# An event list that sets the order of every instruction of a fused attention and two-MLP kernel

## The chip, the cores and the metric

The kernel runs on one NeuronCore of a Trainium2 chip. The metric is the device time of one execution in microseconds (us). The engines are TensorE (PE in the profile, its weight loads PEld), VectorE (DVE), ScalarE (ACT), GpSimd (POOL) and SyncE (SP), which issues most transfers.

## What is computed

Windowed attention with 8 global keys and a window of 96 over 2 x 8 heads of 768 tokens of 64 elements, then a gated MLP of 2048 inner columns and a second one of 1536. Tokens are 1536, the model width is 512.

```python
scores = scale * np.matmul(q, k.transpose(0, 1, 3, 2)) + bias[None, :, :, :]
scores = np.where(keep, scores, -1000000000.0)
a = np.exp(scores - np.max(scores, axis=-1, keepdims=True))
x = np.matmul(a / (np.sum(a, axis=-1, keepdims=True) + 1e-09), v)   # then [tokens, 512]
h = x @ w_in;  y = (h * sigmoid(h)) @ w_out
z = (sigmoid(y @ w_gate) * (y @ w_val)) @ moe2_w_out
```

The weights come as 64-bit floats. Each MLP product is made of three matmuls of a 32-bit kind (high by high, high by low, low by high).

## The kernel before, in words

Attention works on 12 blocks of 128 tokens and, in each, on 4 pairs of heads: 48 steps n. A step transposes a pair's queries and keys (`emit_T`, two transposes of 128x128, L342), evicts them to the key tile kt (L353 on VectorE or L355 on ScalarE), makes the scores (`emit_QK`, L379: two matmuls, each in one half of the rows of the array, 64*128; each stands as two records in the trace), reduces them with a mask (`soft`, L394 on VectorE), exponentiates (L401, ScalarE), normalises (L407, L408 on VectorE, L413 on GpSimd), transposes the weights of the values (`emit_PT`, L430, evicted at L434) and multiplies with the values (`emit_PV`, L451, each in one half of the columns, 128*64). `take` (L459) evicts a finished block of tokens to X, a high part on ScalarE and a low part on VectorE.

A weight tile is loaded raw (`dma_w`, L176), made 32-bit on ScalarE and VectorE (`to_f32`, L156 to L161), and split into a high and a low part (L169, L170). `pump_w` spaces these out by a count of units; tiles w0 to w15 exist from the start, w16 to w23 only after attention's memory is given back.

The MLP's matmuls all go through `mm3` (L505) or L682 and L684. While attention runs, `window` (L599) puts ten macros of the first MLP between attention's units. The table PLAN lists them as (token group, first inner chunk, columns, first column, attention slots); four have 256 columns, six have 512. A macro makes 24 matmuls into the inner banks H, then an activation, then 24 into the output bank Y (one bank, bank 7, evicted by VectorE at L589 and L591 to acc). `phase_rest` (L632) does the rest of both MLPs. Before any macro, `run_att` (L622) runs six units of attention alone and puts three warm-up matmuls on a tile of zeros (`warm_up`, L895) after each.

What sets the order: the code is written in the order of these units, and the framework's scheduler, which works with its own estimate of durations, then orders the instructions of each engine. Only for later score and value matmuls is TensorE's order given by hand (`tc.manual_schedule`, in `att_units`, L477). Tiles come from pools, and the framework adds the waits.

Of the kernel before, what the change touches and what calls it, by code (L numbers as in the profile page):

```python
# [8 lines left out]
F32 = mybir.dt.float32  # L9
# [16 lines left out]
NEG = 1.0e30  # L26
# [4 lines left out]

@with_exitstack
def attn_moe_moe2_kernel(
# [14 lines left out]
    nc = tc.nc  # L48
    B, H, S, D = q.shape
# [15 lines left out]
    stage_p = fast.enter_context(tc.tile_pool(name="stage", bufs=3))  # L65
    u_p = fast.enter_context(tc.tile_pool(name="up", bufs=2))
    g_p = fast.enter_context(tc.tile_pool(name="gp", bufs=4))
    e_p = fast.enter_context(tc.tile_pool(name="ep", bufs=2))
# [10 lines left out]
    nc.gpsimd.memset(pad, 0.0)  # L79
    W = [main.tile([128, 2, 512], F32R, name=f"w{n}") for n in range(16)]  # L80

# [71 lines left out]
    def to_f32(st, raw):  # L153
        lw, hw = raw[:, :, 0], raw[:, :, 1]
        ui = st.bitcast(I32)
        nc.scalar.activation(out=st, in_=hw.bitcast(F32), func=AF.Copy, scale=2.0 ** -112)  # L156
        nc.vector.tensor_scalar(ui, ui, 3, None, op0=ALU.logical_shift_left)
        nc.vector.scalar_tensor_tensor(  # L158
            out=ui, in0=lw, scalar=29, in1=ui, op0=ALU.logical_shift_right, op1=ALU.bitwise_or
        )  # L160
        nc.vector.scalar_tensor_tensor(  # L161
# [3 lines left out]
    def split_w(n):  # L165
        w = W[n % 24]
        st = u_p.tile([128, 512], F32, tag="u", name="u")
        to_f32(st, stages.pop(n))
        nc.scalar.activation(out=w[:, 0, :], in_=st, func=AF.Copy)  # L169
        nc.vector.tensor_tensor(w[:, 1, :], st, w[:, 0, :].bitcast(F32), ALU.subtract)  # L170

    def load_raw(st, s):
        o = st.rearrange("p f t -> p (f t)")
        if len(s.shape) == 3:
            o = o.rearrange("p (a f) -> p a f", f=256)
        nc.sync.dma_start(out=o, in_=s)  # L176

    def dma_w(n):
        st = stage_p.tile([128, 512, 2], I32, tag="stage", name="stage")
# [34 lines left out]
    qk_p = att.enter_context(tc.tile_pool(name="qkp", bufs=2))  # L214
    v_p = att.enter_context(tc.tile_pool(name="vp", bufs=3))
    t_p = att.enter_context(tc.tile_pool(name="tp", bufs=5))
    pt_p = att.enter_context(tc.tile_pool(name="ptp", bufs=3))
# [3 lines left out]
    ssum = [ap1.tile([128, 2], F32, name=f"ssum{i}") for i in range(4)]  # L221

    def load_n():
        raw = ap1.tile([128, 2, 2], I32, name="nraw")
        nc.sync.dma_start(out=raw[:, 0, :], in_=n_global.bitcast(I32).partition_broadcast(128))
        nc.scalar.dma_start(out=raw[:, 1, :], in_=n_local.bitcast(I32).partition_broadcast(128))
        return raw

    def make_n(raw):
        f = ap1.tile([128, 2, 2], F32, name="nf")  # L230
        neg = ap1.tile([128, 2, 1], F32, name="nneg")
        nc.vector.tensor_copy(f, raw)
        nc.vector.tensor_scalar(neg, f[:, :, 0:1], 0.0, None, op0=ALU.is_lt)
        nc.vector.tensor_tensor(neg, neg, f[:, :, 1:2], ALU.add)
        nc.vector.scalar_tensor_tensor(
# [3 lines left out]
        nc.vector.tensor_scalar(nval[:, 2:3], nval[:, 1:2], -1.0, None, op0=ALU.mult)  # L239

    def scratch():
        return t_p.tile([128, 2, 256], F32, tag="t", name="t").rearrange("p a b -> p (a b)")
# [3 lines left out]
    def make_iota():  # L246
        t = scratch()
        ri = t.bitcast(I32)
        nc.gpsimd.iota(ri[:, 0:128], pattern=[[-1, 128]], base=0, channel_multiplier=1)
        nc.gpsimd.iota(ri[:, 128:256], pattern=[[-1, 128]], base=128, channel_multiplier=1)  # L250
        nc.gpsimd.iota(ri[:, 256:384], pattern=[[1, 128]], base=0, channel_multiplier=0)
        f = scratch()
        nc.vector.tensor_copy(f[:, 0:384], ri[:, 0:384])
# [4 lines left out]
    def make_mask0():  # L258
# [703 lines left out]
```

## Time and profile before

| | before |
| --- | --- |
| device time, median of 3 (lowest to highest) | 682.52 us (682.02 to 682.7) |
| the profiled execution | 681.75 us, of which the span of the instructions 680.0 |
| granted TensorE clock, mean | 0.995 |
| TensorE busy | 667.6 us, 3463 records |
| VectorE busy | 374.2 us |
| ScalarE busy | 277.9 us |
| GpSimd busy | 84.6 us |

Busy times are unions of records. A matmul's record lasts longer than the distance to the next one, so TensorE's pace is read from starts: in a line of the timeline, n records of one shape that start at A and are followed by another line at B took B - A together.

### The profile page before, as it was taken

How to read it: one execution, taken by the hardware profiler on the slowest of the kernel's cores; microseconds unless marked ns; L12 is line 12 of the kernel's file. 1: busy time of each engine (PE TensorE's matmuls, PEld its weight loads, DVE VectorE, ACT ScalarE, POOL GpSimd, SP SyncE). 2: the span in 40 equal slices, each digit the busy share in tenths (PEclk: the TensorE clock that was granted, in tenths of full speed). 3: DMA queues.
4: the chain of work that ended last, by engine and by line, in shares of the span. 5: the costliest groups of instructions: out<-in, count | busy, mean ns of one | idle time of the engine just before them, and what ended most of it. 6: DMA issues, size and time to landing. Idle time of an engine off the chain costs nothing.

```text
span 680.0 us, 9291 instructions
## 1 busy us (share of the span) xinstructions
PE 667.6 (98%) x3463; PEld 540.1 (79%) x3463; DVE 374.2 (55%) x869; ACT 277.9 (41%) x594; POOL 84.6 (12%) x167
## 2 busy tenths in 40 slices
PE   9999999999999999999999999999999999999996
PEld 7577886777778888888888888888888888888884
DVE  5999975635549999652499941311783311312212
ACT  3797865555546565332366521111452111111110
POOL 4255564343220000000000000000000000000000
PEclk9899999999999999999999999999999999999999
DMA  8666652210004554400025430000250000100101
GB/s 215 174 171 164 171 150 63 48 33 17 17 2 128 182 155 153 125 0 1 24 70 169 141 94 1 0 1 0 63 155 1 1 0 1 62 1 1 62 1 67
DMA packets 65301, 49.05 MB, mean 72 GB/s; under 512 B 39648, under 2 KB 60128, under 8 KB 65248
## 3 DMA queue, kind: packets, MB, share of 16 engines
q1 hardware_dynamic: 64032, 48.11, 24.6%
q8 instruction: 29, 0.48, 0.3%
q10 hardware_dynamic: 1216, 0.26, 0.2%
q14 instruction: 24, 0.20, 0.1%
HBM read 45.22 MB, written 3.15 MB: 71 GB/s over the span
## 4 chain that ended last, share of the span: by engine, by line
PE 93%; DVE 5%; ACT 1%; issue 0%; DVEq 0%
PE bank L505 54%; PE bank L684 14%; PE bank L682 13%; PE bank L379 4%; PE bank L451 3%; PE bank L430 2%; PE bank L897 2%; PE bank L342 1%; DVE t L394 1%; DVE acc L591 1%; DVE w L170 0%; DVE u L158 0%; DVE u L161 0%; DVE acc L703 0%; ACT t L401 0%
## 5 line engine op out<-in xcount | busy, mean ns | idle before, releaser
L505 PE MATMUL bank<-x,w 128*128 128x512 f32 (+1 forms) x1488 | 347.1, 384 | 0.0
L505 PEld LDWEIGHTS bank<-x,w 128*128 128x128 f32 x1488 | 272.6, 188 | 54.4 <-issue 0.8
L542 DVE TENSOR_TENSOR sg<-sg,bank 128x512 f32<-128x512 f32 x36 | 24.7, 687 | 162.5 <-PE bank L505 162.5
L684 PE MATMUL bank<-w,g 128*128 128x512 f32 x432 | 103.9, 389 | 0.0
L684 PEld LDWEIGHTS bank<-w,g 128*128 128x128 f32 x432 | 81.1, 188 | 16.8
L682 PE MATMUL bank<-g,w 128*128 128x512 f32 x384 | 92.4, 389 | 0.0
L682 PEld LDWEIGHTS bank<-g,w 128*128 128x128 f32 x384 | 72.1, 188 | 15.0
L539 ACT ACTIVATE sg<-bank 128x512 f32<-128x512 f32 x36 | 21.6, 599 | 117.3 <-PE bank L505 117.1
L543 ACT ACTIVATE g<-sg 128x512 fp32r<-128x512 f32 x36 | 22.8, 632 | 90.5 <-DVE sg L542 90.5
L156 ACT ACTIVATE u<-stage 128x512 f32<-128x512 f32 x68 | 45.8, 675 | 26.5 <-DVE w L170 26.0
L505 PE MATMUL bank<-g,w 128*128 128x512 f32 (+1 forms) x240 | 53.9, 360 | 2.6 <-DVE acc L591 1.3
L413 POOL TENSOR_SCALAR t<-t,ssum 128x256 f32<-128x256 f32 (+1 forms) x88 | 48.3, 564 | 60.2 <-DVE ssum L408 25.6
L169 ACT ACTIVATE w<-u 128x512 fp32r<-128x512 f32 x68 | 42.5, 629 | 26.2 <-PE bank L505 10.4
L170 DVE TENSOR_TENSOR w<-u,w 128x512 fp32r<-128x512 f32 x68 | 46.9, 692 | 11.4 <-ACT w L169 11.3
L401 ACT ACTIVATE t<-t,nm_all 128x256 f32<-128x256 f32 (+1 forms) x96 | 46.1, 484 | 17.0 <-DVE nm_all L394 17.0
L161 DVE SCALAR_TENSOR_TENSOR u<-stage,u 128x512 int32<-128x512 int32 x68 | 48.2, 709 | 0.3
L158 DVE SCALAR_TENSOR_TENSOR u<-stage,u 128x512 int32<-128x512 int32 x68 | 46.8, 688 | 0.7
L505 PEld LDWEIGHTS bank<-g,w 128*128 128x128 f32 x240 | 38.0, 189 | 10.5 <-DVE acc L591 3.8
L394 DVE CUSTOM_DVE_ANT_0 t<-bank,mask 128x256 f32<-128x256 f32 (+1 forms) x96 | 33.7, 395 | 16.6 <-PE bank L379 15.8
L530 ACT ACTIVATE g<-sg 128x512 fp32r<-128x512 f32 x48 | 30.3, 631 | 22.2 <-DVE sg L529 12.0
L529 DVE SCALAR_TENSOR_TENSOR sg<-sg,bank 128x512 f32<-128x512 f32 x32 | 21.9, 683 | 27.9 <-ACT sg L528 27.9
L528 ACT ACTIVATE sg<-bank 128x512 f32<-128x512 f32 x32 | 19.1, 596 | 39.6 <-PE bank L505 39.2
(91 smaller groups left out, 516.4 us busy)
## 6 DMA issues: line engine op xcount, KB each, us to landing
stage<-in_moe_w_out_dram SPq DMA_DIRECT2D x28, 512.0 KB, 3.6
stage<-in_moe_w_in_dram SPq DMA_DIRECT2D x16, 512.0 KB, 3.7
stage<-in_moe_w_gate_dram SPq DMA_DIRECT2D x12, 512.0 KB, 3.5
stage<-in_moe_w_val_dram SPq DMA_DIRECT2D x12, 512.0 KB, 3.5
v<-in_v_dram SPq DMA_DIRECT2D x12, 256.0 KB, 3.5
out_dram<-acc SPq DMA_DIRECT2D x12, 256.0 KB, 2.0
qk<-in_k_dram SPq DMA_DIRECT2D x11, 256.0 KB, 3.6
qk<-in_q_dram SPq DMA_DIRECT2D x11, 256.0 KB, 3.8
```

What stands on the lines that cost most here:

```text
L156: nc.scalar.activation(out=st, in_=hw.bitcast(F32), func=AF.Copy, scale=2.0 ** -112)
L158: nc.vector.scalar_tensor_tensor(out=ui, in0=lw, scalar=29, in1=ui, op0=ALU.logical_shift_right, op1=ALU.bitwise_or)
L161: nc.vector.scalar_tensor_tensor(out=ui, in0=hw, scalar=-2 ** 31, in1=ui, op0=ALU.bitwise_and, op1=ALU.bitwise_or)
L169: nc.scalar.activation(out=w[:, 0, :], in_=st, func=AF.Copy)
L170: nc.vector.tensor_tensor(w[:, 1, :], st, w[:, 0, :].bitcast(F32), ALU.subtract)
L394: nc.vector.tensor_tensor_reduce(t[:, e, 0:w], sp[e], mask[e][:, m0:m0 + w], op0=ALU.add, op1=ALU.min, scale=-c, scalar=3.0e38, accum_out= ...
L401: nc.scalar.activation(out=t[:, e, 0:w], in_=t[:, e, 0:w], func=AF.Exp, scale=-1.0, bias=nm_all[:, gi, 2 * p + e:2 * p + e + 1], accum_out ...
L413: nc.gpsimd.tensor_scalar(t[:, e, 0:w], t[:, e, 0:w], ss[:, e:e + 1], 1.0, op0=ALU.mult, op1=ALU.mult)
L505: nc.tensor.matmul(ps, wl[(slice(None), a) + wsl], xl[(slice(None), b) + xsl], start=(first and j == 0), stop=(last and j == len(order) - 1),)
L530: nc.scalar.activation(out=gt[:, 0, :], in_=sg, func=AF.Copy)
L682: nc.tensor.matmul(yb[d], w[:, a, sl], gt[:, b, :], start=st, stop=en)
L684: nc.tensor.matmul(yb[d], gt[:, a, sl], w[:, b, :], start=st, stop=en)
```

## The change

The kernel gets a layer `Issue` that records every operation of all five engines instead of handing it to the framework. It stores, for each, the memory it writes and reads, and a duration from formulas by engine, shape and kind (for instance 0.0133 + n/2400 us for a dense matmul of n columns, 0.07 + n/960 for most of VectorE). A table TURN holds what TensorE spends between two shapes. `order` then runs an event list: of all operations whose inputs are ready it takes the one that can start first, and among those within 0.02 us the one recorded first; matmuls in a `together` block stay together. The result is issued on every engine in that order under `manual_schedule`. There are two such lists: one up to the end of `window`, one for `phase_rest`.

With it come smaller edits. Pools become fixed rings of the same numbers of buffers (`ring`). The warm-up matmuls of the units go; instead the event list puts `filler` matmuls wherever it finds TensorE idle for over 0.15 us, one for each 0.115 us, up to the first matmul of `window`. Both pairs' scores and values form one group. The output bank Y becomes two banks (7 and 4) for the last macros, when transposes of queries and keys are done, and three in the second list.

```diff
+TURN = {"fr": 0.095, "fc": 0.097, "tr": 0.095, "tc": 0.097, "rf": 0.192, "cf": 0.148, "rt": 0.247, "ct": 0.203,
+        "rc": 0.195, "cr": 0.147, "tf": -0.082}
...
+        while any(cand.values()):
+            best = None
+            for e, cs in cand.items():
+                if cs:
+                    at = [(max(free[e], max(m.ready for m in g)), p, i, g) for p, i, g in cs]
+                    s = min(a[0] for a in at)
+                    a = min((a for a in at if a[0] <= s + 0.02), key=lambda a: a[1:3])
+                    if best is None or a[0] < best[0]:
+                        best = a[0], e, a
+            at, e, (_, prio, i, g) = best
+            cand[e].remove((prio, i, g))
+            if e == "tensor" and self.filling:
+                self.filling = not g[0].stop_fill
+                if self.filling:
+                    done += [filler] * max(0, int((at - free[e] - 0.15) / 0.115))
...
             if n < TIE:
-                emit_PV(n - 4)
-                emit_PV(n - 3)
-                sp = [emit_QK(n), emit_QK(n + 1)]
+                with en.together():
+                    emit_PV(n - 4)
+                    emit_PV(n - 3)
+                with en.together():
+                    sp = [emit_QK(n), emit_QK(n + 1)]
             else:
-                with tc.manual_schedule(engines={mybir.EngineType.PE}):
-                    sp = [emit_QK(n + 1), emit_QK(n)][::-1]
+                with en.together():
+                    sp = [emit_QK(n), emit_QK(n + 1)]
+                    emit_PV(n - 4)
                     emit_PV(n - 3)
-                    emit_PV(n - 4)
...
-            yb = bk["Y"][0]
+            yb = bk["Y"][(d // 2 if two else d) % len(bk["Y"])]
...
+            if n0 > NBLK * NP // 2:
+                bk["Y"] = [bank[7], bank[4]]
...
-            warm_up(3)
...
         prev = window(START)
+        assert not deferred
+        en.issue(filler)
...
+        bk["Y"] = [bank[7], bank[4], bank[3]]
+        en.begin()
         phase_rest(prev)
         flush()
+        en.issue(filler)
```

In the listed orders below, L235 is the one line that issues for all after the change; names are tiles with their numbers. The first place is TensorE at the program's start, the first transposes of queries and keys (qk) into banks 4 and 6. Before, 28 warm-up pairs stand ahead of these rows:

```order
L342 MATMUL bank4_80<-ident_84,qk_153 128x128
L897 LDWEIGHTS warm_140
L897 MATMUL bank5_81<-warm_140 128x256
L342 MATMUL bank4_80<-ident_84,qk_153 128x128
L897 LDWEIGHTS warm_140
L897 MATMUL bank5_81<-warm_140 128x256
L342 MATMUL bank6_82<-ident_84,qk_153 128x128
```

After, 50 stand ahead:

```order
L235 MATMUL bank4_68<-ident_72,qk0_128 128x128 x2
L1138 LDWEIGHTS warm_127
L1138 MATMUL bank5_69<-warm_127 128x256
L1138 LDWEIGHTS warm_127
L1138 MATMUL bank5_69<-warm_127 128x256
L235 MATMUL bank6_70<-ident_72,qk0_128 128x128 x2
```

What moved: the transposes stand in pairs, and 22 more warm-up matmuls stand ahead of them.

The second place is TensorE some units later, still ahead of the macros: scores into banks 0 and 1 (one for each head of a pair), values into bank 3. Before:

```order
L451 MATMUL bank3_79<-pt_495,v_173 64x128 x2
L451 MATMUL bank3_79<-pt_495,v_178 64x128 x2
L430 MATMUL bank2_78<-ident_84,t_480 128x128 x2
L451 MATMUL bank3_79<-pt_521,v_173 64x128 x2
L451 MATMUL bank3_79<-pt_521,v_178 64x128 x2
L379 MATMUL bank0_76<-kt0_128 128x256
L379 MATMUL bank0_76<-kt1_129 128x256
L430 MATMUL bank2_78<-ident_84,t_480 128x128 x2
L379 MATMUL bank1_77<-kt0_128 128x256
L379 MATMUL bank1_77<-kt1_129 128x256
```

After:

```order
L235 MATMUL bank0_64<-kt2_117 128x256
L235 MATMUL bank1_65<-kt2_117 128x256
L235 MATMUL bank0_64<-kt3_118 128x256
L235 MATMUL bank1_65<-kt3_118 128x256
L235 MATMUL bank3_67<-pt1_139,v0_130 64x128 x2
L235 MATMUL bank3_67<-pt1_139,v1_131 64x128 x2
L235 MATMUL bank3_67<-pt2_140,v0_130 64x128 x2
L235 MATMUL bank3_67<-pt2_140,v1_131 64x128 x2
L235 MATMUL bank2_66<-ident_72,t1_134 128x128 x4
L235 MATMUL bank4_68<-ident_72,qk1_129 128x128 x2
```

What moved: the scores of both banks alternate and are followed at once by the values; before, the two matmuls of bank 0 stood apart from those of bank 1, with transposes between them.

The third place is VectorE around the split of w12, the weight of the plan's row (0, 6, 512): reductions (ISA t), steps of conversion (u), normalisation (ssum), blocks of tokens (x). Before:

```order
L161 SCALAR_TENSOR_TENSOR u_1156<-stage_984,u_1156 128x512
L157 TENSOR_SCALAR u_1200<-u_1200 128x512
L407 TENSOR_SCALAR ssum0_136<-ssum0_136 128x2
L158 SCALAR_TENSOR_TENSOR u_1200<-stage_1050,u_1200 128x512
L353 TENSOR_SCALAR kt3_131<-bank4_80 128x256
L408 RECIPROCAL ssum0_136<-ssum0_136 128x2
L407 TENSOR_SCALAR ssum1_137<-ssum1_137 128x2
L161 SCALAR_TENSOR_TENSOR u_1200<-stage_1050,u_1200 128x512
L170 TENSOR_TENSOR w12_107<-u_1156,w12_107 128x512
L408 RECIPROCAL ssum1_137<-ssum1_137 128x2
L526 SCALAR_TENSOR_TENSOR sg_1082<-sg_1082,bank5_81 128x512
L170 TENSOR_TENSOR w13_108<-u_1200,w13_108 128x512
```

After:

```order
L235 TENSOR_TENSOR x1_76<-bank3_67,x1_76 128x4x128
L235 TENSOR_SCALAR ssum2_125<-ssum2_125 128x2
L235 SCALAR_TENSOR_TENSOR u0_102<-stage0_99,u0_102 128x512
L235 RECIPROCAL ssum2_125<-ssum2_125 128x2
L235 TENSOR_SCALAR ssum3_126<-ssum3_126 128x2
L235 TENSOR_SCALAR u1_103<-u1_103 128x512
L235 RECIPROCAL ssum3_126<-ssum3_126 128x2
L235 SCALAR_TENSOR_TENSOR u1_103<-stage1_100,u1_103 128x512
L235 TENSOR_TENSOR w12_95<-u0_102,w12_95 128x512
L235 SCALAR_TENSOR_TENSOR u1_103<-stage1_100,u1_103 128x512
L235 TENSOR_SCALAR kt1_116<-bank4_68 128x2x128
L235 COPY acc0_78<-bank7_71 128x2x256
```

What moved: ahead of w12's split now stands the eviction of a block of tokens of the second token group (x1), behind it a key tile and an eviction to acc, and steps that wait for each other (u, ssum) stand closer together.

## Rows read from the trace of the kernel before

**Rows 1.** Head of the page: busy us (share of the span) xinstructions.

```profile
PE 667.6 (98%) x3463; PEld 540.1 (79%) x3463; DVE 374.2 (55%) x869; ACT 277.9 (41%) x594; POOL 84.6 (12%) x167
```

**Rows 2.** Busy time by stretch; columns as in the first row.

```profile
core 0: us, PE busy (x) PEld busy (x) DVE busy (x) ACT busy (x) POOL busy (x), PEclk, DMA share, GB/s
5.80:28.00 22.20, 21.54 (x157) 14.62 (x155) 17.50 (x80) 13.60 (x46) 8.21 (x25) 1.00 0.89 227
28.00:41.40 13.40, 12.78 (x88) 8.86 (x88) 13.26 (x53) 11.41 (x35) 6.02 (x14) 0.87 0.77 183
41.40:92.70 51.30, 50.37 (x410) 42.16 (x409) 49.72 (x144) 40.59 (x104) 29.70 (x42) 1.00 0.59 167
92.70:216.10 123.40, 121.02 (x774) 92.74 (x773) 70.29 (x222) 67.24 (x177) 38.97 (x77) 1.00 0.19 47
216.10:672.80 456.70, 456.70 (x2016) 378.16 (x2015) 220.50 (x368) 143.78 (x235) 0.00 (x0) 1.00 0.18 56
```

**Rows 3.** Timeline, 0 to 20 us: start us, us, engine, line, operation, tiles, count.

```profile
1.04 5.03 PE L897 MATMUL bank<-warm 128*128 128x256 bf16 x28 [1.04 <-DVE warm L900]
...
5.91 0.27 PE L342 MATMUL bank<-ident,qk 128*128 128x128 f32 x1
...
7.00 2.02 PE L897 MATMUL bank<-warm 128*128 128x256 bf16 x17
...
8.62 0.35 DVE L278 TENSOR_SCALAR mask<-mask 128x128 f32<-128x128 f32 x1
...
10.37 0.29 DVE L394 CUSTOM_DVE_ANT_0 t<-bank,mask 128x128 f32<-128x128 f32 x1 [1.07 <-PE bank L379]
```

**Rows 4.** Timeline of TensorE, 20 to 75 us: scores L379, values L451, transposes L342, L430.

```profile
38.51 1.13 PE L379 MATMUL bank<-kt 64*128 64x256 f32 x4
39.56 0.44 PE L430 MATMUL bank<-ident,t 128*128 128x128 f32 x2
...
53.89 1.13 PE L379 MATMUL bank<-kt 64*128 64x256 f32 x8
54.96 0.44 PE L342 MATMUL bank<-ident,qk 128*128 128x128 f32 x2
...
58.21 0.38 PE L342 MATMUL bank<-ident,qk 128*128 128x128 f32 x2
58.52 1.09 PE L451 MATMUL bank<-pt,v 128*64 128x128 f32 x16
59.55 0.66 PE L430 MATMUL bank<-ident,t 128*128 128x128 f32 x4
```

**Rows 5.** Timeline of TensorE, 88 to 110 us: dense matmuls are L505.

```profile
91.08 2.01 PE L505 MATMUL bank<-x,w 128*128 128x512 f32 x8
...
107.11 0.44 PE L342 MATMUL bank<-ident,qk 128*128 128x128 f32 x2
107.30 0.37 PE L505 MATMUL bank<-g,w 128*128 128x256 f32 x1
...
108.60 0.44 PE L342 MATMUL bank<-ident,qk 128*128 128x128 f32 x2 [0.71 <-ACT kt L355]
109.33 0.96 PE L505 MATMUL bank<-g,w 128*128 128x512 f32 x3 [0.29 <-DVE acc L591]
```

**Rows 6.** Timelines of VectorE, 41 to 62 and 230 to 242 us.

```profile
57.29 0.41 DVE L394 CUSTOM_DVE_ANT_0 t<-bank,mask 128x256 f32<-128x256 f32 x1
57.64 0.08 DVE L394 DVE_READ_ACCUMULATOR2_ANT nm_all<- 128x1 f32 x1
57.64 0.68 DVE L170 TENSOR_TENSOR w<-u,w 128x512 fp32r<-128x512 f32 x1
58.24 0.68 DVE L158 SCALAR_TENSOR_TENSOR u<-stage,u 128x512 int32<-128x512 int32 x1
...
239.89 0.69 DVE L158 SCALAR_TENSOR_TENSOR u<-stage,u 128x512 int32<-128x512 int32 x1
240.61 0.69 DVE L161 SCALAR_TENSOR_TENSOR u<-stage,u 128x512 int32<-128x512 int32 x1
```

**Rows 7.** Busy time by stretch, 28.7 to 32.1 us; columns as in rows 2.

```profile
28.70:32.10 3.40, 3.40 (x16) 2.74 (x16) 3.40 (x12) 1.49 (x6) 1.24 (x3) 0.50 0.45 147
```

More of the change, by code (lines that the diff above doesn't have):

```diff
@@ L1 @@
-from contextlib import ExitStack
+from contextlib import ExitStack, contextmanager
+from itertools import cycle
 import concourse.bass as bass
@@ new lines, in region @@
+def region(a):
+    ps, pc = list(a.ap)[0]
+    free = [(st, c) for st, c in list(a.ap)[1:] if c > 1]
+    p0, f0 = (a.offset // ps, a.offset % ps) if ps else (0, a.offset)
+    free.sort(key=lambda e: -abs(e[0]))
+    width = 1
+    while free and abs(free[-1][0]) <= width:
+        st, c = free.pop()
+        width = max(width, (c - 1) * abs(st) + width)
+    runs = [f0]
+    for st, c in free:
+        runs = [r + k * st for r in runs for k in range(c)]
+    return a.name, a.space, p0, p0 + pc, tuple((r, r + width) for r in sorted(runs))
@@ new lines, with __init__, __getattr__, call @@
+class Engine:
+    def __init__(self, issue, name):
+        self.issue, self.name = issue, name
+    def __getattr__(self, meth):
+        real = getattr(getattr(self.issue.nc, self.name), meth)
+        def call(*args, **kw):
+            iss = self.issue
+            if not iss.on:
+                return real(*args, **kw)
+            o = Op(self.name, meth, args, kw)
+            o.prio = len(iss.ops) + iss.bias
+            o.stop_fill = iss.stop_fill
+            iss.ops.append(o)
+            if iss.open is not None and self.name == "tensor":
+                iss.open.append(o)
+                o.group = iss.open
+        return call
@@ L32, in attn_moe_moe2_kernel, with ring @@
+def ring(pool, shape, dt, name, n):
+    return cycle([pool.tile(shape, dt, name=f"{name}{i}") for i in range(n)])
 @with_exitstack
@@ L175, in load_raw @@
             o = o.rearrange("p (a f) -> p a f", f=256)
-        nc.sync.dma_start(out=o, in_=s)
+        en.sync.dma_start(out=o, in_=s)
     def dma_w(n):
-        st = stage_p.tile([128, 512, 2], I32, tag="stage", name="stage")
+        st = next(stage_r)
         load_raw(st, wsrc[n])
@@ L503, in mm3 @@
     def mm3(ps, wl, wsl, xl, xsl, first, last, order=((0, 0), (0, 1), (1, 0))):
-        for j, (a, b) in enumerate(order):
-            nc.tensor.matmul(
-                ps, wl[(slice(None), a) + wsl], xl[(slice(None), b) + xsl],
-                start=(first and j == 0), stop=(last and j == len(order) - 1),
-            )
+        with en.together():
+            for j, (a, b) in enumerate(order):
+                en.tensor.matmul(
+                    ps, wl[(slice(None), a) + wsl], xl[(slice(None), b) + xsl],
+                    start=(first and j == 0), stop=(last and j == len(order) - 1),
+                )
     def h_units(g, key, ps, cols=slice(0, G), free=True):
@@ L892, in attn_moe_moe2_kernel, with filler @@
     main2 = {}
-    warm = ap1.tile([128, 256], BF16, name="warm")
-    def warm_up(n):
-        for _ in range(n):
-            nc.tensor.matmul(bank[5][:, 0:256], warm[:, 0:128], warm, start=True, stop=True)
+    def filler():
+        nc.tensor.matmul(
+            bank[5][:, 0:256].rearrange("p (a b) -> p a b", a=2), warm, warm2, start=True, stop=True
+        )
     with ExitStack():
         nc.vector.memset(warm, 0.0)
-        warm_up(11)
+        make_identity(nc, ident)
+        en.begin()
         load_qk(0)
-        make_identity(nc, ident)
         make_iota()
```

488 lines of the change are left out of this document (326 added, 162 removed).

## The prediction, made before the change was run

> **What bounds the kernel now.** I read the head of the profile's page first [rows 1], then the table of busy time by stretch [rows 2], then stretches of the timeline of TensorE and VectorE. It says TensorE busy 98%, which looks like a kernel with nothing left. The table cuts it into three. From 216.1 us to the last matmul at 672.8 TensorE is busy in every microsecond: 2016 matmuls, 0.2267 us apart (456.7 / 2015), each a 512-column one that has to be done. The change cannot shorten that stretch or the 7.2 us behind it (680.0 - 672.8: last evictions and stores). Before 216.1 the work is mixed, and there "busy" hides three things: warm-up matmuls that compute nothing, turns between shapes, and waits that are shorter than a matmul's own 0.27 to 0.4 us, since records overlap.
>
> VectorE is the other bound. It is busy 13.26 of 13.40 us from 28 to 41.4 and 49.72 of 51.30 from 41.4 to 92.7, 97% together, and 70.29 of 123.40 after that [rows 2]. So up to about 92.7 TensorE can go no faster than VectorE gives it weights, masks and scores; from there on it is limited by its own list and by single waits.
>
> **What the change does to TensorE's list.** The computation is the same; only order and warm-up count change. I counted both listed orders whole.
>
> Turns: the 96 score matmuls stand in 35 runs before and 24 after, the value matmuls in 31 runs and 24, and 20 of these follow a score run directly. Two transposes take 0.31 us from start to start if value matmuls follow (58.21 to 58.52, [rows 4]) and 0.19 if a dense one does (107.11 to 107.30, [rows 5]): entering costs 0.12. Leaving is inside the run: 8 score records 1.07 (53.89 to 54.96), 16 value records 1.03 (58.52 to 59.55).
>
> Unpaired scores: a row of x4 in which both matmuls of one half of the array stand together takes 1.05 us (38.51 to 39.56), as much as x8 in both halves (53.89 to 54.96). Half of that is lost, some 0.43 us each, and the list before has about eight such runs; the new groups keep the halves side by side. That is 3.4 us, all of it before 92.7.
>
> Warm-up: 101 matmuls become 111, and of these 50 instead of 28 stand ahead of the first transpose. The 28 ran from 1.04 to 5.9, over 0.17 us each, the later 17 at 0.11 ((2.02 - 0.27) / 16) [rows 3]. So 22 more cost 2.4 us at the head: first transposes at 8.3 instead of 5.91. This is partly covered: the first score reduction before came only at 10.37, and VectorE had finished its mask only at 8.97 (8.62 + 0.35, [rows 3]). VectorE is idle 4.7 of the 22.2 us up to 28 [rows 2]; I let that idle time take up the late head and cost it at nothing, bounds 0 and 2.4.
>
> **The sum, over one place in the program.** I take the first matmul of the plan's row (0, 6, 512), with weight w12. It is the last of the eight at 91.08 (91.08 + 7 x 0.2267 = 92.7, [rows 5]). After it the lists differ by counting:
> - 24 fewer 256-column matmuls, half of 0.2267 each with overhead, 0.12: 2.9 us;
> - 30 fewer transposes at 0.10 (0.19 / 2, [rows 5]): 3.0;
> - 16 fewer score records, two runs of 1.07: 2.1;
> - 40 fewer value records, 2.5 runs of 1.03: 2.6;
> - 6 fewer entries at 0.12, and 9 value runs that are entered straight from scores, about 0.12 each: 1.8.
>
> Together 12.4 us less work behind w12, because attention is further along there. Then waits: two transposes ahead of a dense matmul take 0.19 (107.11) but 0.73 where the single output bank still waits for VectorE (108.60 to 109.33) [rows 5]. Seven such waits between 92.7 and 216.1 lose 3.4 us, one for a key tile 0.9. The change gives two or three output banks late in this stretch and lets other groups go first; I credit 2.5 of the 4.3, bounds 0 and 4.3. Behind w12: 580.1 - 12.4 - 2.5 = 565.2 us.
>
> When does w12 start? By VectorE: what it must have done by then, followed through the waits of both lists, is 48 score reductions before and 60 after (of them 8 and 16 short), 13 and 15 key tiles, 5 and 6 token blocks, two more output evictions, five more normalisations, and four steps of weight conversion less (1.9 together). Starts in the saturated stretch lie 0.35 apart behind a reduction and 0.60 behind a 512-wide operation [rows 6]. So 4 x 0.35 + 8 x 0.21 (estimate, the same less 128 columns) + 2 x 0.33 + 0.6 + 1.2 + 5 x 0.25 - 1.9 = 4.9 us more, at 97% busy 5.0: w12 at 97.7. By TensorE alone: 92.7 + 10.6 (the work done earlier) + 2.4 (late head) - 3.4 (pairs) - 2.8 (turns) - about 7 = 92.5. The 7 are an estimate: priced by [rows 3 to 5], the list up to w12 takes some 85 of the 91.7 us from 1.04, and the rest is waits and the stretch at half clock [rows 7]. VectorE decides, 97.7.
>
> Sum: 97.7 + 565.2 + 7.2 = 670.1 us of span against 680.0, 9.9 less. The profiled execution took 681.75, so 671.9; the median shown is 682.52, 0.8 above that execution: **672.6 us**. The stretch of dense work after it keeps its order, and its 97% to 100% cover is unchanged, so I cost it at nothing.
>
> **A price for VectorE's order.** The new list has 24 neighbours on VectorE up to w12 of which the second waits for the first, against 13. Such a pair is 0.72 apart (239.89 to 240.61) where an independent one is 0.60 (57.64 to 58.24) [rows 6]: 11 x 0.12 = 1.3 us more, at most. The Trainium skill (VectorE: DVE Perf Modes, The DRAIN you can't avoid) says that chaining without semaphores saves nothing, a wait between two operations being free; by it the 1.3 us are zero. The trace speaks against it by the 0.12. I leave the 1.3 in the range, since some of the pairs lie in the idle head.
>
> **Rivals.**
> 1. VectorE does not bind: the new list lets reductions and conversions fill VectorE's idle time before 28 us (4.7 of 22.2 us, [rows 2]) and w12 comes at TensorE's 92.5, with one more microsecond of later waits gone. Then 6 less: about 666. For it: VectorE idles early. Against: the conversions that could fill it need weights that are loaded behind the attention's own inputs. Read by the page's 98% alone this rival could not be, since TensorE is idle only 12.4 us (680.0 - 667.6, [rows 1]). The Trainium skill (Trainium Kernel Development and Optimization, Best Practices) says to judge the distance to the limit by the share of weight loads, not by matmul busy time; that is 79% here [rows 1], and by it more than 12.4 may be won. The starts above side with it: they show turns and waits inside busy time. Chance 0.24.
> 2. The gain is given back: the head's 2.4 us and the 1.3 us pass through, VectorE runs as before, so w12 comes at 101.4, and none of the later waits goes: 101.4 + 567.7 + 7.2 = 676.3 of span, about 679. Chance 0.14.
> 3. Slower: the granted clock. From 28.7 to 32.1 it was 0.50, which is 1.2 instead of 2.4 GHz [rows 7], after TensorE's starts had drawn apart. If waiting for VectorE brings this back again and again between 30 and 98 us, each such 3.4 us takes 1.7 us of work away. The first three vanish in the 5.2 us by which TensorE is ahead of VectorE there; to reach 684 it takes about ten. One was seen, with gaps of the same kind. Chance 0.05.
> 4. The change does not do what it says: the list is fixed at build time, and where durations come out otherwise each engine waits in order for the late one; the turns saved come back as waits and the time stays within 1 us of 682.5. Chance 0.04.
>
> The forecast has 0.53.
>
> **How the numbers follow.** Forecast 672.6, its own spread 668 to 677. The range 663 to 680 leaves out the clock rival, the fourth and the tail of the first. A difference of 0.2% (1.4 us) is what a measurement of this kernel can tell from none: faster 0.89 (0.53 + 0.24 + most of rival 2), same 0.05, slower 0.06.
>
> **What would show it.** In the profile after: 50 warm-up matmuls ahead of the first transpose, which starts near 8.3; score rows of x8, or x16 followed at once by value rows, no x4 that takes 1.05; VectorE idle early and then over 95% busy to about 95 us; w12's first matmul near 98 us; the last transposes and value matmuls earlier than before by some 20 us; dense rows 0.2267 apart from there with no gap. Wrong if w12 starts before 94 (rival 1) or after 101 (rival 2), if a granted clock of 0.50 shows after 35 us (rival 3), or if gaps open behind 200 us.

## The result, and the profile after

The changed kernel takes **675.12 us** (median of 4 runs, 674.78 to 675.86), the kernel before 682.61 in the same session: a ratio of 0.9891, 95% interval 0.9874 to 0.9908. That is 7.5 us less, where 9.9 were forecast; the predicted 672.6 lies 2.5 us below the median, and the range 663 to 680 holds it. The profiled execution took 674.92 us, its span is 673.1.

The head of the page of after, which answers [rows 1] (busy us, share of the span, instructions):

```profile
PE 658.4 (98%) x3473; PEld 538.4 (80%) x3473; DVE 375.0 (56%) x869; ACT 276.9 (41%) x594; POOL 87.5 (13%) x167
```

Every engine does what it did; only TensorE's busy time fell, by 9.2 us, at ten matmuls more. Its 98% is the same share as before, so this row alone shows nothing of the change but the span. The table of busy time by stretch, cut at places that answer [rows 2]:

```profile
core 0: us, PE busy (x) PEld busy (x) DVE busy (x) ACT busy (x) POOL busy (x), PEclk, DMA share, GB/s
28.00:36.20 8.20, 6.97 (x65) 5.39 (x64) 7.28 (x31) 6.45 (x20) 3.76 (x8) 1.00 0.73 197
36.20:102.00 65.80, 61.60 (x531) 51.93 (x530) 61.34 (x192) 54.62 (x149) 38.85 (x59) 1.00 0.60 162
102.00:210.00 108.00, 107.30 (x664) 83.27 (x663) 60.93 (x189) 55.70 (x141) 34.36 (x62) 1.00 0.16 39
210.00:666.60 456.60, 456.60 (x2017) 378.33 (x2015) 225.18 (x374) 145.02 (x238) 0.00 (x0) 1.00 0.18 58
```

The last row is the dense stretch, as long as in [rows 2] (456.60 against 456.70), and its last matmul starts 6.2 us earlier. The half clock of [rows 7] has not come back: the granted clock is 1.00 in every row. Ahead of the dense stretch the roles have moved: from 102 to 210 TensorE is idle 0.7 of 108.0 us, where it was idle 2.4 of 123.4; from 36.2 to 102 it is now idle 4.2 us, and VectorE is busy 93% of that stretch, not 97%.

The place that the sum was built on, w12's first matmul, and the last group of dense matmuls, from the timeline of TensorE in after (start us, us, operation, tiles, count):

```profile
101.81 0.95 PE L235 MATMUL bank<-x,w 128*128 128x512 f32 x3
...
658.66 8.32 PE L235 MATMUL bank<-w,g 128*128 128x512 f32 x36
```

w12 starts at 101.81, not at 97.7; the prediction had named a start after 101 as a sign against it. The last matmul starts at 658.66 + 35 x 0.2267 = 666.6, so 564.8 us behind w12, where 565.2 were forecast, and 6.5 us remain behind it, where 7.2 were. The whole miss is ahead of w12.

The head of after, timeline of TensorE, which answers [rows 3]:

```profile
0.97 8.49 PE L1138 MATMUL bank<-warm 128*128 128x256 bf16 x50 [0.97 <-DVE warm L1143]
9.30 0.38 PE L235 MATMUL bank<-ident,qk 128*128 128x128 f32 x2
...
11.95 1.47 PE L1138 MATMUL bank<-warm 128*128 128x256 bf16 x12
```

And of VectorE:

```profile
7.79 0.29 DVE L235 TENSOR_TENSOR mask<-mask,t 128x128 f32<-128x128 f32 x1
10.15 0.42 DVE L235 TENSOR_SCALAR kt<-bank 128x256 f32<-128x256 f32 x1 [2.08 <-PE bank L235]
10.50 0.21 DVE L235 COPY mask<-mask 128x120 f32<-128x120 f32 x1
10.74 0.23 DVE L235 TENSOR_SCALAR mask<-mask 128x128 f32<-128x128 f32 x1
...
11.56 0.29 DVE L235 CUSTOM_DVE_ANT_0 t<-bank,mask 128x128 f32<-128x128 f32 x1 [0.59 <-PE bank L235]
```

The 50 warm-up matmuls end at 9.3 us, a microsecond later than forecast; VectorE has run out of work by 8.08 and waits 2.08 us for the first transposes. The first reduction comes 1.19 us later than before.

The microsecond belongs to this execution. In the four runs below that also have 50 warm-up matmuls ahead, the first transposes start at 7.90, 8.11, 8.38 and 8.49. What differs is when the warm-up matmuls double their pace. TensorE in after (us, busy, matmuls, granted clock):

```profile
5.80:6.30 0.50, 0.50 (x5) 1.00 0.62 142
```

The same half microsecond in the run that starts them at 8.11 (a conversion step less, below):

```profile
5.80:6.30 0.50, 0.50 (x7) 1.00 0.79 179
```

Seven to half a microsecond is the pace of that run from 4.8 us on, and of after only from 7.3; the row of the granted clock says 1.00 in both.

The groups are as the order said. One stretch of the same timeline, which answers [rows 4]:

```profile
57.77 1.14 PE L235 MATMUL bank<-kt 64*128 64x256 f32 x8
58.83 1.09 PE L235 MATMUL bank<-pt,v 128*64 128x128 f32 x16
```

Scores stand in eight records, values follow at once, and the row of four that took 1.05 us is gone.

### The profile page after: what moved, and what is told of

It is laid out like the page before. It is cut to its first block, busy times and chain, and to the rows that moved or that the text cites. A ratio compares the mean times of both kernels' runs of the same rounds, so it can differ in the third digit from the quotient of the medians.

```text
span 673.1 us, 9430 instructions
## 1 busy us (share of the span) xinstructions
PE 658.4 (98%) x3473; PEld 538.4 (80%) x3473; DVE 375.0 (56%) x869; ACT 276.9 (41%) x594; POOL 87.5 (13%) x167
## 4 chain that ended last, share of the span: by engine, by line
PE 88%; DVE 6%; ACT 2%; issue 2%; POOL 1%; ACTq 0%; DVEq 0%; POOLq 0%
PE bank L235 87%; DVE u L235 2%; PE bank L1138 2%; ACT t L235 2%; DVE t L235 2%; DVE acc L235 1%; DVE w L235 1%; POOL t L235 0%; POOL g L235 0%; DVE ssum L235 0%; ACT pt L235 0%; DVE x L235 0%; DVE kt L235 0%; ACT x L235 0%; DVE sg L235 0%
## 5 line engine op out<-in xcount | busy, mean ns | idle before, releaser
L235 PE MATMUL bank<-x,w 128*128 128x512 f32 (+1 forms) x1488 | 349.6, 385 | 0.7 <-DVE x L235 0.7
L235 PEld LDWEIGHTS bank<-x,w 128*128 128x128 f32 x1488 | 272.0, 188 | 54.0 <-DVE x L235 0.9
L235 PE MATMUL bank<-g,w 128*128 128x512 f32 (+1 forms) x624 | 145.4, 377 | 0.7 <-DVE acc L235 0.7
L235 PEld LDWEIGHTS bank<-g,w 128*128 128x128 f32 x624 | 110.2, 188 | 21.2 <-DVE acc L235 0.9
L235 DVE TENSOR_TENSOR sg<-sg,bank 128x512 f32<-128x512 f32 x36 | 24.7, 686 | 161.9 <-PE bank L235 161.9
L235 ACT ACTIVATE sg<-bank 128x512 f32<-128x512 f32 x84 | 49.9, 593 | 150.1 <-PE bank L235 148.9
L235 PE MATMUL bank<-w,g 128*128 128x512 f32 x432 | 103.5, 389 | 0.0
L235 ACT ACTIVATE g<-sg 128x512 fp32r<-128x512 f32 x84 | 53.0, 631 | 106.5 <-DVE sg L235 106.4
L235 DVE SCALAR_TENSOR_TENSOR u<-stage,u 128x512 int32<-128x512 int32 x136 | 94.2, 699 | 1.6
L235 PEld LDWEIGHTS bank<-w,g 128*128 128x128 f32 x432 | 81.1, 188 | 16.8
L235 POOL TENSOR_SCALAR t<-t,ssum 128x256 f32<-128x256 f32 (+1 forms) x88 | 52.4, 607 | 64.4 <-DVE ssum L235 25.5
L235 ACT ACTIVATE u<-stage 128x512 f32<-128x512 f32 x68 | 45.9, 677 | 34.7 <-DVE w L235 28.6
L235 DVE TENSOR_TENSOR g<-sg,g 128x512 fp32r<-128x512 f32 x68 | 46.9, 689 | 23.4 <-ACT g L235 23.1
L235 DVE SCALAR_TENSOR_TENSOR sg<-sg,bank 128x512 f32<-128x512 f32 x48 | 32.8, 682 | 46.0 <-ACT sg L235 46.0
L235 ACT ACTIVATE t<-t,nm_all 128x256 f32<-128x256 f32 (+1 forms) x96 | 46.0, 481 | 26.0 <-DVE nm_all L235 25.4
L235 ACT ACTIVATE w<-u 128x512 fp32r<-128x512 f32 x68 | 42.6, 630 | 33.9 <-DVE u L235 19.2
L235 DVE TENSOR_TENSOR w<-u,w 128x512 fp32r<-128x512 f32 x68 | 46.7, 693 | 11.0 <-ACT w L235 10.9
L235 DVE CUSTOM_DVE_ANT_0 t<-bank,mask 128x256 f32<-128x256 f32 (+1 forms) x96 | 33.1, 397 | 15.5 <-PE bank L235 11.7
L235 DVE TENSOR_TENSOR acc<-acc,bank 128x512 f32<-128x512 f32 x48 | 32.0, 682 | 10.5 <-PE bank L235 10.5
L235 DVE TENSOR_SCALAR u<-u 128x512 int32<-128x512 int32 x68 | 30.1, 445 | 4.3 <-ACT u L235 3.4
L235 ACT ACTIVATE pt<-bank 128x512 f32<-128x512 f32 (+1 forms) x48 | 26.3, 551 | 12.2 <-PE bank L235 12.2
L235 PE MATMUL bank<-ident,t 128*128 128x128 f32 x176 | 27.7, 277 | 2.4 <-ACT pt L235 2.0
```

The lines of the kernel that those rows point to most:

```text
L235: getattr(getattr(self.nc, o.eng), o.meth)(*o.args, **o.kw)
```

## The experiments

Differences of 1.4 us or less between two kernels are at the edge of what the intervals tell apart; each is given as the ratio to the kernel before, and where a difference is that small, the verdict rests on the trace.

### Fewer warm-up matmuls at the head

```diff
-                    done += [filler] * max(0, int((at - free[e] - 0.15) / 0.115))
+                    done += [filler] * min(28, max(0, int((at - free[e] - 0.15) / 0.115)))
```

> The changed kernel, but of the warm-up matmuls that the event list puts into one gap at most 28 stand, so 28 instead of 50 ahead of the first transpose (89 in all instead of 111). Theory (the late head passes through to w12, since VectorE's idle time before 28 us cannot be used by anything else): first transposes at 6 to 7 us instead of 9.3, w12's first matmul 1 to 1.5 us earlier than 101.8, time about 673.8. Rival (VectorE's idle time takes the head up, as the prediction had it): first transposes as early, but w12 within 0.3 us of 101.8 and the time within 0.4 us of the changed kernel's 675.1.

Measured: 672.75 us, ratio 0.9852 (0.9837 to 0.9867). The event list gives warm-up matmuls no time of their own, so the order of everything else is the same and only the head is shorter. Timeline of TensorE of this kernel:

```profile
0.97 4.79 PE L1138 MATMUL bank<-warm 128*128 128x256 bf16 x28 [0.97 <-DVE warm L1143]
5.60 0.38 PE L235 MATMUL bank<-ident,qk 128*128 128x128 f32 x2
...
99.20 0.94 PE L235 MATMUL bank<-x,w 128*128 128x512 f32 x3
```

Transposes come 3.7 us earlier, w12 2.6, the time falls by 2.4, more than the theory said. Of the 3.7, 1.0 to 1.4 is the slow start of the execution of after shown above. From w12 to the last matmul both kernels take 564.8 us. The theory holds, and the prediction's "at nothing" falls. How much VectorE's idle time takes up can be read with a third trace: in the run with one output bank (below), whose order up to w12 is that of after, the same 50 warm-up matmuls ended earlier, transposes started at 7.90 and w12 at 100.41. From 9.30 to 7.90 all 1.4 us come through, from 7.90 to 5.60 some 1.2 of 2.3. So about 1.1 us of a late head is absorbed, and the rest is not.

### Is it VectorE? A conversion step less, and one more

The step of the conversion that adds the lowest three bits, left out for the first 16 weights or made twice (here twice):

```diff
-        en.vector.scalar_tensor_tensor(
-            out=ui, in0=lw, scalar=29, in1=ui, op0=ALU.logical_shift_right, op1=ALU.bitwise_or
-        )
+        for _ in range(2 if twice else 1):
+            en.vector.scalar_tensor_tensor(
+                out=ui, in0=lw, scalar=29, in1=ui, op0=ALU.logical_shift_right, op1=ALU.bitwise_or
+            )
```

> The changed kernel without one step in the conversion of each of the first 16 weights: the step on VectorE that adds the lowest three bits of the 32-bit number is left out, so these weights are slightly less exact. It takes 16 operations of 128x512 off VectorE ahead of w12, 16 x 0.60 = 9.6 us, 13 to 14 of them before w12 and 8 us there, and nothing off TensorE. Theory (VectorE sets when w12 starts): w12's first matmul at about 94 instead of 101.8, time about 668. Rival (TensorE's own list or ScalarE's evictions of the value weights set it): w12 at most 1.5 us earlier, time 673.5 or more.

> The changed kernel with the same step of the conversion (the one that adds the lowest three bits) made twice for each of the first 16 weights, which leaves the numbers as they are: 16 more operations of 128x512 on VectorE, each waiting for the one before it, 0.60 to 0.72 us, 9.6 to 11.5 us in all, some 13 of them before w12. Nothing more on TensorE. Theory (VectorE sets the pace up to w12, and taking work off it only uncovered the next bound): the added work comes through nearly whole, time 682 to 685. Rival (TensorE and its waits for ScalarE set it as much as VectorE): half of it or less comes through, as the 5.5 us of 9.6 did when the step was left out, time 680 or less.

Measured: left out 669.61 us (0.9807, 0.9794 to 0.982), 5.5 less than the changed kernel; made twice 681.33 (0.9979, 0.997 to 0.9989), 6.2 more. In time both fall between theory and rival: of 9.6 us of VectorE's work (the second step, which waits for the first, may take up to 11.5) some six tenths come through, whichever way it goes. w12 moved less: to 99.42, where the theory had 94 and the rival 100.3 or later, and to 105.81; the first transposes of these executions, at 8.11 and 8.49, stand ahead of those of after. The event list also orders anew: without the step 8 score and 8 value records more stand ahead of w12, so that less remains behind it. Busy time from 28 us to w12, of after:

```profile
28.00:101.81 73.81, 68.38 (x593) 57.13 (x592) 68.43 (x220) 60.88 (x168) 42.61 (x67) 1.00 0.61 166
```

Without the step:

```profile
28.00:99.42 71.42, 68.86 (x605) 58.14 (x602) 60.83 (x211) 61.73 (x174) 36.77 (x68) 1.00 0.64 172
```

With the step made twice:

```profile
28.00:105.81 77.81, 69.49 (x572) 55.87 (x571) 76.11 (x231) 59.44 (x161) 40.65 (x63) 0.98 0.58 157
```

VectorE (third pair) is idle 5.4, 10.6 and 1.7 us in the three. With the step twice it is busy 98% of the stretch; without the step the time saved becomes idle time, in which VectorE waits for TensorE and ScalarE (4.7 and 4.9 us). The changed kernel stands between, and there TensorE is as busy as VectorE: 68.38 against 68.43 us of 73.81. So VectorE is a bound, but not alone, and the 97% that the prediction multiplied by is reached only with more work on it. (With the step twice the granted clock also fell to 0.70 between 48 and 52 us in the profiled execution, which is part of the 6.2.)

### Turns alone, in the kernel before

```diff
-TIE = 16
+TIE = 0
```

> The kernel before, with one number changed: TIE = 0, so that the hand-written TensorE order of scores and values holds from the first unit and not only from step 16. Score runs fall from 35 to 27, value runs from 31 to 24, and no score run stands in one half of the array alone: about 7 us less on TensorE's list, nearly all of it ahead of w12, nothing less on VectorE. Theory (VectorE sets w12 there): w12 stays at 91 to 93 us, and the time falls by at most 2 to 3 us, to 680 or more. Rival (TensorE's list sets it, so the turns alone are the gain): w12 at about 86, time about 675.5, the whole gain of the changed kernel.

Measured: 684.1 us, ratio 1.0023 (1.0014 to 1.0032): a little slower, with what was estimated as some 7 us less on TensorE's list. w12's first matmul starts at 94.39: not at the rival's 86, and later than the theory's 91 to 93. Busy time of this kernel from 28 us and from its start up to there:

```profile
28.00:94.39 66.39, 59.93 (x494) 48.59 (x493) 63.00 (x197) 54.12 (x145) 36.08 (x58) 1.00 0.64 170
0.00:94.39 94.39, 85.12 (x678) 68.16 (x678) 82.77 (x285) 69.50 (x191) 46.65 (x95) 0.98 0.71 183
```

Of the kernel before, up to its w12:

```profile
28.00:92.69 64.69, 63.14 (x494) 51.01 (x494) 62.97 (x196) 51.99 (x138) 35.72 (x55) 0.97 0.63 170
```

Two rows of TensorE's timeline in the kernel with TIE = 0:

```profile
29.34 1.13 PE L379 MATMUL bank<-kt 64*128 64x256 f32 x8 [0.77 <-DVE kt L353]
...
34.85 1.13 PE L379 MATMUL bank<-kt 64*128 64x256 f32 x8 [0.79 <-DVE kt L353]
```

From 28 us on TensorE is busy 59.93 us, 3.2 less than over the same stretch of before, but about 1.7 of that is the half clock of [rows 7], which in this run came ahead of 28 us (granted clock 0.57 from 24 to 28). Counted from the start, at a mean clock of 0.98 in both, TensorE is busy 4.3 us less (85.12 against 89.44, the row of before below) and VectorE 0.9 more (82.77 against 81.85). The time that TensorE saves becomes waits, of which 2.8 of 6.3 us are for key tiles that VectorE evicts in its queue behind other work. Fewer turns by themselves bring nothing in the order before. That w12 follows VectorE there fits, but is not shown apart: with this order VectorE too waits longer (3.4 us against 1.7 from 28 us on).

### Work moved off VectorE

Key tiles to ScalarE in every step; and, with at most 28 warm-up matmuls to a gap, the low part of every second weight to GpSimd:

```diff
-            if n % 2:
+            if False:
...
-        en.vector.tensor_tensor(w[:, 1, :], st, w[:, 0, :].bitcast(F32), ALU.subtract)
+        eng = en.gpsimd if n < 16 and n % 2 else en.vector
+        eng.tensor_tensor(w[:, 1, :], st, w[:, 0, :].bitcast(F32), ALU.subtract)
```

> The changed kernel with every key tile evicted by ScalarE instead of every second one: some 15 operations of 0.33 us, 5 us, less on VectorE up to w12 and some 4 us more on ScalarE, which is busy 54.6 of 65.8 us between 36.2 and 102 us. Theory (VectorE is the bound, ScalarE has room): w12 3 to 4 us earlier, time about 672. Rival (the evictions on ScalarE are already what transposes wait for): w12 no earlier than 101, time 674.5 to 677.

> The kernel whose gaps take at most 28 warm-up matmuls (672.75 us), with the last step of the conversion (the low part, 128x512) of every second of the first 16 weights on GpSimd: 8 operations, 0.60 us each, 4.8 us less on VectorE, and 8 of about 1.2 us each, or 10 us, more on GpSimd, which is busy 38.9 of 65.8 us between 36.2 and 102. Theory (0.6 us of time for each us taken off VectorE, as in the two runs with the step left out and made twice): 2.5 to 3 us less, time about 670. Rival (GpSimd becomes late with the normalisation of scores, or both engines slow each other): time 672.5 or more.

Measured: key tiles on ScalarE 674.15 us (0.9877, 0.9862 to 0.9892), not to be told from the changed kernel. w12 starts at 104.08, no earlier than 101 as the rival had it, with 8 score and 8 value records more ahead of it; the time lies just below the rival's 674.5, and the theory's 672 did not come. Low parts on GpSimd 677.26 (0.9926, 0.991 to 0.9943), 4.5 more than its base: the rival. A group of GpSimd's instructions in this run between 28 and 210 us (count, busy us, mean ns, idle before and what ended it):

```profile
L235 POOL TENSOR_TENSOR w<-u,w 128x512 fp32r<-128x512 f32 x7 | 9.2, 1311 | 15.9 <-ACT w L235 6.7 <-DVE u L235 5.6 <-DVE kt L235 3.6
```

The same step on VectorE in this run:

```profile
L235 DVE TENSOR_TENSOR w<-u,w 128x512 fp32r<-128x512 f32 x11 | 9.2, 834 | 0.0
```

And in its base:

```profile
L235 DVE TENSOR_TENSOR w<-u,w 128x512 fp32r<-128x512 f32 x18 | 12.9, 719 | 0.0
```

The means hide the cost. Of the 11 steps on VectorE nine took 0.67 to 0.69 us, and two 1.28 and 1.79 (in the base one of 18 took 1.23 and one 0.85). One of the two long ones and the step that runs on GpSimd beside it:

```profile
40.28 1.28 DVE L235 TENSOR_TENSOR w<-u,w 128x512 fp32r<-128x512 f32 x1
39.73 1.28 POOL L235 TENSOR_TENSOR w<-u,w 128x512 fp32r<-128x512 f32 x1
```

Three more 128x512 steps of VectorE stand beside a moved step like this, and took 1.66, 1.22 and 1.82 us where steps of their kinds took 0.68, 0.42 and 0.68 in most places. The four together are 3.5 us longer, of the 4.8 (8 x 0.60) that were taken off. The head of the page of this run:

```profile
PE 655.7 (97%) x3454; PEld 535.7 (79%) x3454; DVE 375.2 (56%) x861; ACT 277.0 (41%) x594; POOL 91.0 (13%) x175
```

And of its base:

```profile
PE 655.0 (98%) x3451; PEld 535.3 (80%) x3451; DVE 374.8 (56%) x869; ACT 277.0 (41%) x594; POOL 88.2 (13%) x167
```

With eight instructions fewer VectorE is busy as long: the move took nothing off it. The Trainium skill (Perfetto Trace Analysis, Optimizing Scalar/DVE Operations) warns that moving operations from VectorE to GpSimd may not help, since the two share a read port. The four long steps agree with it. GpSimd also stood idle 15.9 us ahead of the seven steps of its row above, waiting for their inputs in its order. How the 4.5 us divide between the two was not tested.

### One output bank

```diff
-                bk["Y"] = [bank[7], bank[4]]
+                bk["Y"] = [bank[7]]
...
-        bk["Y"] = [bank[7], bank[4], bank[3]]
+        bk["Y"] = [bank[7]]
```

> The changed kernel with a single output bank Y (bank 7) throughout, as before the change. Theory (the prediction's credit of 2.5 us for waits behind w12 is what the second and third bank bring): w12 as in the changed kernel, behind it 567 to 568 us instead of 564.8, time 677 to 678. Rival (the waits went because the event list puts other work into them): behind w12 within 0.5 us, time 674.6 to 675.7.

Measured: 677.2 us (0.9921, 0.9906 to 0.9936), 2.1 more. Timeline of TensorE of this kernel:

```profile
100.41 0.95 PE L235 MATMUL bank<-x,w 128*128 128x512 f32 x3
...
194.73 1.65 PE L235 MATMUL bank<-g,w 128*128 128x512 f32 x6 [0.97 <-DVE acc L235]
197.25 1.62 PE L235 MATMUL bank<-g,w 128*128 128x512 f32 x6 [0.87 <-DVE acc L235]
...
659.94 8.32 PE L235 MATMUL bank<-w,g 128*128 128x512 f32 x36
```

Behind w12 it is 659.94 + 7.93 - 100.41 = 567.5 us against 564.8. The theory holds: 2.7 us come back, most of it as waits for VectorE's eviction to acc just below 200 us, where the changed kernel starts the same matmuls without one. The 2.5 credited were about right, and the banks brought them.

### No warm-up matmuls after the head

```diff
-                    done += [filler] * max(0, int((at - free[e] - 0.15) / 0.115))
+                    done += [filler] * (min(28, max(0, int((at - free[e] - 0.15) / 0.115))) if not any(d is filler for d in done) else 0)
```

> The changed kernel with 28 warm-up matmuls ahead of the first transpose and none later, to be set against the run that caps each gap at 28 (89 warm-up matmuls, 672.75 us, first transposes at 5.60, w12 at 99.2). Theory (the later 61 stand only where TensorE waits anyway, and the granted clock does not need them): time 672.2 to 673.3, granted clock 1.00 from 8 us on. Rival 1 (they keep the granted clock up): a stretch of half clock as in rows 7 after 8 us, which takes 1.7 us of work for each 3.4 us, time 674.5 or more. Rival 2 (they come in the way of work that is ready before the event list thinks so): w12 1 us or more earlier, time below 671.8.

Measured: 674.13 us (0.9867, 0.9852 to 0.9882), 1.4 more than with 89. The intervals overlap, but the trace says the same: w12 starts at 100.75 against 99.20, and behind it both take 564.8 us. Of the 1.55 us, 0.3 are there at the first transposes (5.92 against 5.60). Busy time of TensorE by stretch (us, busy, matmuls, granted clock):

```profile
8.00:12.00 4.00, 1.69 (x16) 0.96 1.06 274
12.00:16.00 4.00, 3.91 (x21) 0.61 1.09 333
...
28.00:32.00 4.00, 1.68 (x14) 1.00 0.88 234
32.00:36.00 4.00, 4.00 (x31) 0.57 0.68 186
```

Two rows of its timeline:

```profile
11.39 0.98 PE L235 MATMUL bank<-kt 64*128 64x128 f32 x8 [1.74 <-ACT kt L235]
...
30.17 0.44 PE L235 MATMUL bank<-ident,qk 128*128 128x128 f32 x2 [1.75 <-DVE kt L235]
```

Twice the granted clock goes to 1.2 GHz (0.61 and 0.57 are means over a stretch that is partly at half), each time behind a row in which TensorE was busy 1.69 or 1.68 of 4.00 us. With warm-up matmuls in these waits, in the first experiment, the granted clock is 1.00 in every such row from 8 us to w12, for instance:

```profile
32.00:36.00 4.00, 3.29 (x34) 1.00 0.65 184
```

Two such stretches should have cost 3.4 us by the price of [rows 7]; at most 1.4 came through. Rival 1 in kind, less in size.

### One duration for every operation

```diff
+        self.occ = {"tensor": 0.19, "vector": 0.43, "scalar": 0.47, "gpsimd": 0.51, "sync": 0.42}[self.eng]
+        self.lat = self.occ
...
-TURN = {"fr": 0.095, "fc": 0.097, "tr": 0.095, "tc": 0.097, "rf": 0.192, "cf": 0.148, "rt": 0.247, "ct": 0.203,
-        "rc": 0.195, "cr": 0.147, "tf": -0.082}
+TURN = {}
```

> The kernel with 28 warm-up matmuls and no later ones, with one duration for every operation of an engine (the mean by the page: TensorE 0.19, VectorE 0.43, ScalarE 0.47, GpSimd 0.51 us, SyncE 0.42; the formula for transfers stays) and no turn costs in the event list. The groups that stay together are the same, so score and value runs are 24 each as before. Theory (what the measured durations bring is that each engine meets its inputs when they are ready): TensorE's waits up to 200 us grow by 5 us or more, w12 or what follows it comes later, time 677 or more. Rival (any list that takes what can start first is nearly as good, and the groups make the gain): within 1.5 us of the run without later warm-up matmuls.

> One duration for every operation of an engine and no turn costs, as in the run that took 702.85 us, but with the event list's warm-up matmuls, at most 28 to a gap (28 at the head, 155 in all). In that run TensorE's granted clock was at half for most of the time between 12 and 30 us. Theory (the order is what is bad, the clock is a consequence of its waits): TensorE still waits for key tiles and value weights between 40 and 200 us, time 692 or more. Rival (half clock without warm-up matmuls made most of the 28 us): granted clock 1.00 from 8 us on, time 682 or less.

> The kernel whose gaps take at most 28 warm-up matmuls (672.75 us), with all measured durations but an empty table of turn costs. Runs of scores and values stay 24 each, since the groups make them; 18 instead of 20 value runs are entered straight from scores. Theory (the table only shifts the event list's clock by about 0.2 us a unit, which the waits absorb): time 672 to 674.5. Rival (engines meet their inputs so closely that 0.1 to 0.2 us a turn, some 10 us over attention, opens waits): 676 or more.

Measured: 702.85 us (1.0278, 1.0256 to 1.0301) without later warm-up matmuls, 703.15 (1.031, 1.0288 to 1.0332) with them, and 672.16 (0.9848, 0.9833 to 0.9863) where only the turn costs were taken out. Waits of TensorE with one duration and warm-up matmuls, 40 to 102 us (waited for: us, times, longest):

```profile
PE bank L236 <- ACT pt L236: 5.8, 4, 2.0
PE bank L236 <- DVE acc L236: 2.9, 1, 2.9
PE bank L236 <- DVE kt L236: 2.9, 3, 1.4
```

Its busy time in two stretches:

```profile
40.00:60.00 20.00, 15.22 (x136) 1.00 0.42 120
60.00:80.00 20.00, 15.44 (x134) 1.00 0.55 148
```

TensorE idles a quarter of the time at full clock; in the changed kernel the same view has 2.0 us for value weights (pt), 0.7 for acc and none for key tiles (kt) on VectorE. The order is what is bad, not the clock: theory and not rival. With the same groups and the same rule it takes 28.7 us more than the kernel with measured durations (702.85 against 674.13, both without later warm-up matmuls). The turn costs in the table bring nothing that can be measured: 0.9848 without them, 0.9852 with them.

### The two edits that seemed to help, together

```diff
-                    done += [filler] * max(0, int((at - free[e] - 0.15) / 0.115))
+                    done += [filler] * min(20, max(0, int((at - free[e] - 0.15) / 0.115)))
...
-            if n % 2:
+            if False:
```

> The two edits that brought something, together: at most 20 warm-up matmuls to a gap (20 at the head, 92 in all) and every key tile evicted by ScalarE. Theory (the two gains add: the head passes through to w12, and ScalarE's evictions give 1 us as before): first transposes at 4.5 to 5.6 us, where the run with 28 had 5.60, time 670.8 to 672. Rival (the inputs of the first transposes are not there before 5.5, and with fewer warm-up matmuls the granted clock comes back to half): first transposes at 5.5 or later or a row of half clock between 8 and 36 us, time 672.5 or more.

Measured: 672.31 us (0.9851, 0.9833 to 0.9869), no better than the shorter head alone. Timeline of TensorE of this run:

```profile
5.12 0.46 PE L235 MATMUL bank<-ident,qk 128*128 128x128 f32 x2
...
10.97 1.07 PE L235 MATMUL bank<-kt 64*128 64x128 f32 x8 [1.86 <-ACT kt L235]
```

Its busy time in one stretch:

```profile
12.00:16.00 4.00, 4.00 (x28) 0.67 1.02 310
```

The transposes gained 0.5 us, and behind the wait of 1.86 us the granted clock went to half for a while (0.67). The rival's half clock showed, at a time that does not decide. The shorter head, 672.75, is the plain improvement on both kernels; 672.16 and 672.31 can't be told from it.

## Why the prediction was right, and where its sizes were off

- **Turns, pairs and the work behind w12: right.** 12.4 us of work and 2.5 us of waits were taken off the 580.1 us behind w12: forecast 565.2, measured 564.8. The run with one bank confirmed the 2.5 by itself, at 2.7.
- **VectorE decides when w12 starts: right in part.** Rival 1, w12 at 92.5, is out, and with fewer turns the kernel before did not move w12 forward. But the prediction had TensorE 5.2 us ahead of VectorE up to w12, and in the changed kernel TensorE is as busy there as VectorE. Of VectorE's work only some six tenths come through in time, and less at w12; with the key tiles taken off VectorE w12 even came later, behind more of attention.
- **The late head, costed at nothing: the step that failed.** Its upper bound of 2.4 us was the size: that is what the shorter head gives back. In the two traces it is 2.6 at w12, of which 1.0 is bad luck: the 50 warm-up matmuls of that execution ran a microsecond longer than forecast, the longest of the five traces that have them. The reasoning took the end of VectorE's mask work in [rows 3] as cover. That row belongs to the old order; in the new one the mask work that the first scores do not need stands behind the first key tile, so VectorE is free at 8.08 and waits. The cover named in the trace of before was undone by the same change, but for about 1.1 us.
- **VectorE's work and its 97%: off by 1.5 us.** The forecast of 97.7 stands for 86.75 us of VectorE busy (81.85 and 4.9) and 10.94 idle. With the shorter head it is busy 87.42 up to w12 and idle 11.78 (rows below), so 0.7 and 0.8 more; the long head adds the other 2.6 of the 4.1 us by which w12 missed. Whether the 0.7 is the price of dependent neighbours (bound 1.3) was not tested. The counts behind the 4.9 are of what w12 needs, and what VectorE had done by then, by the trace, differs: 52 reductions in before and not 48, three key tiles more and not two, six steps of conversion fewer and not four. That the sum came so close is partly luck. Busy time from the program's start to w12, of before:

```profile
0.00:92.69 92.69, 89.44 (x675) 69.21 (x676) 81.85 (x280) 66.87 (x184) 45.61 (x91) 0.98 0.68 178
```

Of after:

```profile
0.00:101.81 101.81, 93.92 (x796) 76.63 (x796) 87.55 (x306) 76.04 (x217) 53.19 (x105) 1.00 0.64 170
```

With the shorter head:

```profile
0.00:99.20 99.20, 90.52 (x773) 73.86 (x774) 87.42 (x306) 76.22 (x217) 53.69 (x105) 1.00 0.65 174
```

- **Rival 2, gain given back, was half true.** w12 came where it put it (101.4), and behind the 101 that was to be its sign, though by a slow start: the same order reached w12 at 100.41 in another execution. The later waits went all the same. Rival 3 (granted clock) did not occur in the changed kernel behind the head, and the run without later warm-up matmuls shows why: they stand in the waits that would have brought it. Its price was wrong in both directions: it let the first three stretches cost nothing and each later one 1.7 us, while the first two cost at most 0.7 each.
- **The sum.** w12 4.1 late, 0.4 less behind it, 0.7 less in the tail: a span of 673.1 instead of 670.1. Between the profiled execution and the median there were 0.2 us and not 0.8, which leaves 2.5.

## What to carry to other kernels

An order worked out ahead is worth what its durations are worth: the same rule with one duration per engine lost 28 us, while the fine print (turns between shapes of 0.1 to 0.2 us) did not matter. When a step is "covered" by work on another engine, look whether the change moves that work too before costing it at nothing. And where two engines share a bound, neither edit gives its full size: 9.6 us off VectorE gave 5.5, and fewer turns on TensorE gave nothing in the old order.

## What the runs showed of the hardware

- The same 50 warm-up matmuls at the head led to the first transposes at 9.30 us in one profiled execution and 7.90 in another, and w12 moved by the same 1.4 us. Two traces of one order can differ by that much from the start. The pace of the same warm-up matmuls doubles at different times, while the granted clock reads 1.00 throughout.
- VectorE steps of 128x512 that took 0.68 us in most places took 1.28 to 1.82 in four places of one run, each beside a 128x512 step with two inputs on GpSimd.
- Behind waits of 1.7 to 1.9 us on TensorE in the first 36 us the granted clock fell to 1.2 GHz in the run without later warm-up matmuls and in the last one. With up to 28 warm-up matmuls in the waits it stayed at 1.00 up to w12, in the order of the former.
